# Moving elementwise blocks to GpSimd, all DMA issues to SyncE, and transposing both halves of -u at once, in a chunked linear-attention and MLP kernel

## The chip, the cores and the metric

The kernel runs on one core of one Trainium2 chip. The metric is device time in microseconds (us) of one execution; the median of several runs counts. The engines are called as the profile calls them: PE is TensorE (matmuls; PEld is its weight load), DVE is VectorE, ACT is ScalarE, POOL is GpSimd, SP is SyncE, which here only issues DMAs.

## The reference

There are 4 x 8 heads, a sequence of 768 steps and a head dimension of 40. Each head carries a 40 x 40 state through the sequence, and the heads' outputs, side by side, go through an MLP of 320 -> 2048 -> 320. All data is fp32.

```python
for t in range(S):
    y[:, :, t] = np.einsum('bhd,bhde->bhe', rt, state)
    Sa = np.einsum('bhde,bhe->bhd', state, at)
    state_decay = state * wt[:, :, None, :] - np.einsum('bhd,bhe->bhde', Sa, bt)
    state = state_decay + np.einsum('bhd,bhe->bhde', vt, kt)
...
h = x @ w_in
sp = np.where(h > 20.0, h, np.log1p(np.exp(np.minimum(h, 20.0))))
g = h * np.tanh(sp)
return (g @ w_out).astype(np.float32)
```

## The kernel before

**Chunks.** The sequence is cut into 12 chunks of C = 64 steps (`nch` is 12). Within a chunk the recurrence becomes matrix products and the inverse of a triangular 64 x 64 matrix for each head, so only the state passes from chunk to chunk. The 32 heads are laid out as two halves (`be`), in each of which two groups of 40 dimensions (`al`) stand at partitions 0 and 64, and 8 blocks along the free axis. Steps run over two groups `g` of 4 blocks.

**Preparation, `pre_a(c, be)`**, 24 times. SP loads w and a (`wa`, L322) and b and k (`bk`, L325). DVE forms running products of w forward (`P`, L343) and backward (`E`, L348), scales a (L346), and b and k (L354). ACT copies a into a block form `ad` (L352). PE multiplies `ad` with `bk`, which holds b, k and 40 columns of identity beside them (L386). From PSUM, ACT writes the blocks that couple a with b into `GP` (L389, L391) and the 40 identity columns into `HA` (L393), and DVE writes the 64 columns that couple a with k into `HA` with a triangular mask on the way (L394), then masks `GP` in place (L397). PE transposes b and k (L410) and ACT copies the result to `bkn` (L412). POOL stores `P` to DRAM (L357), since the MLP's input needs it.

**Inverse, `inv(n)`**, once for two chunks. DVE turns the 32 x 32 diagonal blocks (L420), inverts them by 30 pairs of small instructions that depend on each other (L425, L428), and turns the result back (L430, `TT`). PE forms the off-diagonal blocks (L444, L452). ACT copies six blocks for each half into `bdT` (L466, L467 from `TT`, L468 from PSUM), PE multiplies `HA` by `bdT` (L476) and ACT copies the product to `KT` (L479).

**Step, `step(c)`**, in order of the chunks. POOL loads v in two layouts and r (`step_loads`: `VS` L487, `UVT` L491, `bdr` L494). PE forms u from `VS` and `KT` (L514), ACT writes -u into `UVT` beside v (L517). PE multiplies `UVT` by r (L557) and DVE masks that into `UVQ` (L560). PE transposes each half's v and -u (`step_u`, L528, two sets of 4 per group) and ACT copies them into `UVQ` (L530). The state is transposed too (L544) and copied to `smd` (L546). PE then adds up the new state and y (L586, L591), DVE updates the state (L596, L602), ACT copies y (L598) and POOL stores it (L623).

**The MLP** takes pairs of chunks. SP loads y and `P` (L790, L791), and DVE multiplies them. Each operand is split into a high and a low part, and PE does both products (L814, L835 to L837). ACT applies Mish (L817). SP also loads the MLP weights (L728, L731), which DVE and ACT split in spare time.

**Order.** The whole program is a list of operations with an engine, a planned duration, reads and writes. `Plan.order` places them one by one: each engine takes among the operations that could start within a small window (`LOOK`) after the earliest the one with the highest priority. A priority is the length of the work that follows, plus an entry of the table `PRIO` by kind and chunk. Each engine runs its operations strictly in the order found; planned durations affect only this order. Scratch tiles (`HA`, `bkn`, PSUM banks and others) come from pools whose buffers are taken in the same pass. SBUF of the preparation and of the inverse is given to the MLP when they are done, and much of the MLP's storage opens only at the end of the steps.

**Queues.** SP issues the loads of `wa`, `bk`, the constants, the MLP's weights and inputs, and the output. POOL issues all others. Each engine issues in its own order and waits at the head of it.

Of the kernel before, what the change touches and what calls it, by code (L numbers as in the profile page):

```python
# [62 lines left out]
class Plan:
# [183 lines left out]
def attention(actx, tc, I, yD, pD, nch, M, S, newPS):  # L247
    nc = tc.nc
    V, A, PE, SP, G = nc.vector, nc.scalar, nc.tensor, nc.sync, nc.gpsimd
    ictx, pctx = ExitStack(), ExitStack()  # L250
# [65 lines left out]
    def pre_a(c, be):  # L316
        S.at('ld', c)
        wa, bk, ad = wab[be], bkb[be], adb[be]
        xo, og, ok, oa, oh = (0, 0, 64, 0, 40) if be == 0 else (0, 64, 0, 64, 0)
# [30 lines left out]
        for al in range(2):  # L350
            q = slice(al * 64, al * 64 + 64)
            op('A', 0.62, lambda q=q, al=al: A.copy(ad[q, :, :, al], a[q].rearrange("p (s k t) -> p s k t", k=2, t=32)),  # L352
# [528 lines left out]
```

## Time and profile before

| | us |
|---|---|
| median of 3 runs | 747.21 |
| lowest and highest of them | 744.37, 747.24 |
| profiled execution | 745.79 |
| its span | 744.0 |

The profile is one execution. Its page gives the busy time of each engine over the span; the views by line, by window of time, by wait and the chain of work that ended last come from the same trace. A group's row has the line, engine, operation, tiles (out <- in), shapes and count, then busy time, mean ns of one, and the idle time ahead of it with what ended it. Busy bars of PE and DVE overlap their neighbours, so a mean bar is longer than the step from one to the next. The page's slices (40 of 18.6 us, in tenths) show how the load moves:

```profile
PE   2554698999999999999989999999999999999997
DVE  7999999899999999999368853123113113111110
ACT  4554576867887787888858644234334324323332
POOL 9111013142224223212220000000000000000000
PEclk9778589999999999999999999999999999999999
```

### The profile page before, as it was taken

The page shows a single profiled execution, that of the slowest core. Times are in us where ns is not written, and L with a number is a line of the kernel's source. Part 1 is how long each engine was busy: PE and PEld are TensorE (multiplying, and loading weights), DVE is VectorE, ACT ScalarE, POOL GpSimd, SP SyncE. Part 2 cuts the span into 40 slices and gives each one's busy share as a digit, 9 for nine tenths or more (in the row PEclk, how much of TensorE's full clock was granted, in tenths as well). Part 3 has the DMA queues.
Part 4 walks back from the last instruction along what each step waited for, and adds up shares of the span by engine and source line. Part 5 has one row for each costly group of instructions (what it writes and reads, how often), then busy time and mean ns, then how long its engine had stood idle before and what let it go on. Part 6 is the DMA issues. An engine that isn't in the chain of part 4 may idle for free.

```text
span 744.0 us, 17243 instructions
## 1 busy us (share of the span) xinstructions
PE 678.6 (91%) x7048; PEld 626.0 (84%) x7048; DVE 456.0 (61%) x975; ACT 420.8 (57%) x937; POOL 102.2 (14%) x166
## 2 busy tenths in 40 slices
PE   2554698999999999999989999999999999999997
PEld 1544698998999989999978999898998989999897
DVE  7999999899999999999368853123113113111110
ACT  4554576867887787888858644234334324323332
POOL 9111013142224223212220000000000000000000
PEclk9778589999999999999999999999999999999999
DMA  7533214364444445144587713003004001000100
GB/s 191 171 98 89 64 39 104 77 139 116 107 109 111 101 118 150 37 117 128 123 220 185 206 46 100 0 12 97 14 1 103 18 1 40 19 0 1 36 1 35
DMA packets 58206, 61.81 MB, mean 83 GB/s; under 512 B 25536, under 2 KB 48704, under 8 KB 58128
## 3 DMA queue, kind: packets, MB, share of 16 engines
q1 hardware_dynamic: 49296, 40.94, 19.6%
q0 software_dynamic: 8832, 19.79, 10.8%
q8 instruction: 55, 0.90, 0.5%
q14 instruction: 23, 0.19, 0.1%
HBM read 48.79 MB, written 11.86 MB: 82 GB/s over the span
## 4 chain that ended last, share of the span: by engine, by line
PE 64%; DVE 22%; ACT 7%; issue 4%; DMA 1%; POOL 0%; ACTq 0%; DVEq 0%
PE ps L814 24%; PE ps L835 7%; PE ps L837 7%; PE ps L836 7%; PE ps L557 4%; DVE XL L428 3%; DVE tmp L425 3%; PE ps L386 3%; PE ps L586 3%; DVE P L343 2%; DVE bk L354 2%; PE ps L476 2%; PE ps L528 2%; DVE HA L394 2%; PE ps L591 1%
## 5 line engine op out<-in xcount | busy, mean ns | idle before, releaser
L819 DVE TENSOR_TENSOR gl<-g,gh 128x1024 fp32r<-128x1024 f32 x48 | 58.8, 1225 | 194.9 <-ACT gh L818 188.7
L817 ACT ACTIVATE g<-ps 128x512 f32<-128x512 f32 x96 | 57.0, 597 | 173.6 <-PE ps L814 173.3
L837 PE MATMUL ps<-w_oh,gl 128*128 128x320 f32 x384 | 118.6, 309 | 0.0
L835 PE MATMUL ps<-w_oh,gh 128*128 128x320 f32 x384 | 118.5, 309 | 0.0
L836 PE MATMUL ps<-w_ol,gh 128*128 128x320 f32 x384 | 118.5, 309 | 0.0
L814 PE MATMUL ps<-xh,w_ih 128*128 128x512 f32 x288 | 113.2, 393 | 0.0
L814 PE MATMUL ps<-xh,w_il 128*128 128x512 f32 x288 | 97.7, 393 | 0.0
L386 PE MATMUL ps<-bk,ad 128*128 128x168 f32 x384 | 68.7, 340 | 26.9 <-DVE bk L354 18.2
L386 PEld LDWEIGHTS ps<-bk,ad 128*128 128x128 f32 x384 | 63.8, 215 | 28.8 <-issue 26.5
L814 PE MATMUL ps<-xl,w_ih 128*128 128x512 f32 x192 | 75.4, 393 | 0.0
L836 PEld LDWEIGHTS ps<-w_ol,gh 128*128 128x128 f32 x384 | 72.1, 188 | 2.1
L835 PEld LDWEIGHTS ps<-w_oh,gh 128*128 128x128 f32 x384 | 72.1, 188 | 2.0
L837 PEld LDWEIGHTS ps<-w_oh,gl 128*128 128x128 f32 x384 | 72.1, 188 | 0.0
L814 PEld LDWEIGHTS ps<-xh,w_il 128*128 128x128 f32 x288 | 54.1, 188 | 12.3
L814 PEld LDWEIGHTS ps<-xh,w_ih 128*128 128x128 f32 x288 | 54.2, 188 | 10.6 <-issue 0.2
L428 DVE TENSOR_TENSOR XL<-XL,tmp 128x30 f32<-128x30 f32 (+9 forms) x180 | 58.7, 326 | 2.0
L425 DVE TENSOR_TENSOR tmp<-XL 128x30 f32<-128x30 f32 (+9 forms) x180 | 58.5, 325 | 1.7
L557 PE MATMUL ps<-bdr,UVT 128*128 128x128 f32 x384 | 48.8, 283 | 4.9 <-ACT UVT L517 2.7
L818 ACT CAST gh<-g 128x1024 fp32r<-128x1024 f32 x48 | 50.4, 1050 | 1.5
L557 PEld LDWEIGHTS ps<-bdr,UVT 128*128 128x128 f32 x384 | 46.1, 197 | 6.0 <-ACT UVT L517 3.4
L476 PE MATMUL ps<-bdT,HA 128*104 128x128 f32 x384 | 46.9, 280 | 2.4 <-ACT bdT L468 2.4
L476 PEld LDWEIGHTS ps<-bdT,HA 128*104 128x104 f32 x384 | 44.1, 174 | 4.1 <-ACT bdT L468 2.2
(89 smaller groups left out, 1170.9 us busy)
## 6 DMA issues: line engine op xcount, KB each, us to landing
wa<-in_wa SPq DMA_DIRECT2D x48, 162.5 KB
bk<-in_bk SPq DMA_DIRECT2D x48, 160.0 KB
cv<-in_wi SPq DMA_DIRECT2D x12, 512.0 KB
cv<-in_wo SPq DMA_DIRECT2D x8, 640.0 KB
pD<-P POOLq DMA_DIRECT2D x48, 81.2 KB, 2.5
bdr<-in_rD POOLq DMA_DIRECT2D x24, 160.0 KB, 4.5
UVT<-in_vD POOLq DMA_DIRECT2D x24, 160.0 KB, 4.0
VS<-in_vN POOLq DMA_DIRECT2D x24, 160.0 KB, 4.7
```

The source lines that it names most:

```text
L386: PE.matmul(pv()[:, j], ad[:, s0 + j].rearrange("p k a t -> p (k a t)"), bk[:, s0 + j], start=(j == 0), stop=True, skip_group_check=True)
L425: op('V', (0.16 + m * i * 0.00104), lambda tv=tv, i=i, m=m: V.tensor_tensor(out=tv, in0=X[:, i + 1:32, i:i + 1].broadcast_to([128, m, i]), ...
L428: op('V', (0.16 + m * i * 0.00104), lambda tv=tv, i=i: V.tensor_tensor(out=X[:, i + 1:32, 0:i], in0=X[:, i + 1:32, 0:i], in1=tv, op=ALU.ad ...
L476: PE.matmul(kv()[:, j], ha.t[:, s0 + j], bd[:, o + s0 + j].rearrange("p a t -> p (a t)"), start=(j == 0), stop=True, skip_group_check=True)
L557: PE.matmul(qv()[:, s], UVT[:, g * 4 + s, be * 128:be * 128 + 128], bdr[:, be, g * 4 + s].rearrange("p a t -> p (a t)"), start=(s == 0), s ...
L814: PE.matmul(b.t, w, x, start=(n == 0), stop=(n == 7), skip_group_check=True)
L817: op('A', 0.6, lambda b=b, j=j: A.activation(g.t[:, j], b.t, AF.Mish), r=[b], w=[(g, j)])
L818: op('A', 1.05, lambda: A.copy(gh.t, g.t), r=[(g, 0), (g, 1)], w=[gh])
L819: op('V', 1.226, lambda: V.tensor_tensor(out=gl.t, in0=g.t, in1=gh.t.bitcast(F32), op=ALU.subtract), r=[(g, 0), (g, 1), gh], w=[gl])
L835: PE.matmul(o, gh.t[:, j, t], oh, start=(f == 0 and j == 0), stop=False, skip_group_check=True)
L836: PE.matmul(o, gh.t[:, j, t], ol, start=False, stop=False, skip_group_check=True)
L837: PE.matmul(o, gl.t[:, j, t], oh, start=False, stop=(f == 7 and j == 1), skip_group_check=True)
```

## The change

- GpSimd (POOL) makes the copies of a into `ad`, and the four copies from `TT` into `bdT` (per chunk and half). Both were ACT's.
- `HA` is filled from PSUM by one ACT copy of 104 columns per group, unmasked; a POOL instruction then multiplies its 64 columns by the mask, once for 8 blocks. For this, b and k change places in `bk`, so that the identity and k stand side by side. The mask on `GP` moves from DVE to POOL too.
- All DMAs that POOL issued are issued by SP.
- `UVT` gets a new layout in which -u of both halves stands side by side (v0, u0, u1, v1), so that one transpose does both halves; v comes by a further load by time (`vst`, 22 loads) and a POOL copy into `UVQ`. The load of v in the other layout has 9 blocks for 8.
- Transposes take 104 partitions and give 104 columns instead of 128. `smd` gets 344 columns for 4 x 128.
- The planner counts several buffers that an operation needs from one pool. The table of priorities is new, and each kind and chunk gets an addition to the window (`LOOKS`).

```diff
+AD, BD, HM, GM, DM = 'G', 'G', 'G', 'G', 'S'
+LOOKS = {
...
-                        for b in o.bufs:
-                            if b.t is None:
-                                t = max(t, min((f for f in self.free[b.pool[0]] if f is not None), default=1e9))
+                        for name, n in o.wants():
+                            free = sorted(f for f in self.free[name] if f is not None)
+                            t = max(t, free[n - 1] if len(free) >= n else 1e9)
...
+    QD = SP if DM == 'S' else G
+    copy = lambda e: A.copy if e == 'A' else G.tensor_copy
...
+    used = slice(0, 104)
+    rows = cst[used, 0:104]
+    heads = lambda x: bass.AP(x.tensor, x.offset, [x.ap[0], [104, 4], [64, 2], [1, 40]])
...
-            op('A', 0.62, lambda q=q, al=al: A.copy(ad[q, :, :, al], a[q].rearrange("p (s k t) -> p s k t", k=2, t=32)),
+            op(AD, 0.62 if AD == 'A' else 0.86, lambda q=q, al=al: copy(AD)(ad[q, :, :, al], a[q].rearrange("p (s k t) -> p s k t", k=2, t=32)),
...
-            op('G', 0.52, lambda al=al: G.dma_start(out=pD[c, be, :, al], in_=P.t[al * 64:al * 64 + 40]), r=[P], w=[('pD', c, be, al)],
+            op(DM, 0.52, lambda al=al: QD.dma_start(out=pD[c, be, :, al], in_=P.t[al * 64:al * 64 + 40]), r=[P], w=[('pD', c, be, al)],
...
+            if HM == 'G':
+                o = min(oi, ok)
+                op('A', 0.15 + 0.088 * m, lambda s0=s0, m=m, pv=pv, o=o: A.copy(ha.t[:, s0:s0 + m], pv()[:, 0:m, o:o + 104]), r=[b],
+                   w=[(ha, s0), (ha, s0 + 1)])
+                continue
...
+        if HM == 'G':
+            op('G', 1.37, lambda: G.tensor_tensor(out=ha.t[:, :, oh:oh + 64], in0=ha.t[:, :, oh:oh + 64],
+                                                  in1=maskH.unsqueeze(1).broadcast_to([128, 8, 64]), op=ALU.mult), r=['cst'],
+               w=[(ha, s0 + x) for s0 in (0, 3, 6) for x in (0, 1)])
+        op(GM, 0.423 if GM == 'V' else 0.81, lambda: (V if GM == 'V' else G).tensor_tensor(out=gp.t[:, u0:u0 + 8, 1], in0=gp.t[:, u0:u0 + 8, 1],
...
-                    PE.transpose(pv()[:, j].rearrange("p a b -> p (a b)"), bk[:, s0 + j, xo:xo + 128], ident)
+                    PE.transpose(pv()[:, j], bk[used, s0 + j, xo:xo + 128], rows)
...
+                    op(BD, 0.4 if BD == 'A' else 0.56, lambda bd=bd, q0=q0, us=us, al=al: copy(BD)(bd[q0, :, al, 0:32], TT[q0, us]), r=['TT'], w=[bdk[al * 3]])
+                    op(BD, 0.4 if BD == 'A' else 0.56, lambda bd=bd, q1=q1, us=us, al=al: copy(BD)(bd[q1, :, al, 32:64], TT[q1, us]), r=['TT'], w=[bdk[al * 3 + 1]])
...
+            op(DM, 0.75, lambda q=q, al=al: QD.dma_start(out=UVW[q, :, 0:128], in_=I['vD'][c, al].rearrange("p s x t -> p s (x t)")), w=[('UVv', al, 0), ('UVv', al, 1)], lat=2.9, srv=0.85)
...
+            op(DM, 0.85, lambda q=q, al=al: QD.dma_start(out=bdr[q, :, :, al].rearrange("p b s t -> p (b s) t"), in_=I['rD'][c, al]),
...
+    def step_v(c):
+        if c < nch - 1:
+            S.at('sv', c)
+            for be in range(2):
+                q = slice(be * 64, be * 64 + 64)
+                op(DM, 0.65, lambda be=be, q=q: QD.dma_start(out=vst[q], in_=I['vN'][c, be]), w=[('vst', be)], lat=2.3, srv=0.7)
+                op('G', 1.0, lambda be=be, q=q: G.tensor_copy(UVQ[be][q, :, 64:104], vst[q]), r=[('vst', be)], w=[('V', be, 0), ('V', be, 1)])
...
+            def tr():
+                for s in range(4):
+                    PE.transpose(tv()[:, s], UVT[used, g * 4 + s, 64:192], rows)
+            op('P', 0.357, tr, r=[('u', g), 'UVz', 'cst'], w=[b], mode=128, work=0.347)
             for be in range(2):
...
+                src, dst = slice(be * 64, be * 64 + 64), slice(64 - be * 64, 128 - be * 64)
```

More of the change, by code (lines that the diff above doesn't have):

```diff
@@ L20 @@
 LOOK = 0.05
-LOOKS = {}
-PRIO = {
-    'zero': (-99, -65, 338, 745, 81, -91, -72.5, 60, -47.5, -354, -210, 224.5,),
[27 rows of a table removed]
+AD, BD, HM, GM, DM = 'G', 'G', 'G', 'G', 'S'
+LOOKS = {
+    'zero': (1.5,),
[26 rows of a table added]
+}
+PRIO = {
+    'zero': (341.5, 474.5, 514, 250, 460.5, -15, -63.5, -142.5, 9.5, -240.5, -107.5, -174,),
[28 rows of a table added]
 }
@@ L59, with wants @@
 class Op:
-    pass
+    def wants(self):
+        n = {}
+        for b in self.bufs:
+            if b.t is None:
+                n[b.pool[0]] = n.get(b.pool[0], 0) + 1
+        return n.items()
 class Plan:
@@ L283, in attention @@
     VS = tiles(cs, 2, [128, 2, 344], "VS")
-    UVT = cs.tile([128, 8, 256], F32, name="UVT")
+    UVW = cs.tile([128, 9, 256], F32, name="UVT")
+    UVT = UVW.rearrange("p s x -> p (s x)")[:, 64:2112].rearrange("p (s x) -> p s x", x=256)
+    vst = cs.tile([128, 16, 40], F32, name="vst")
     UVQ = tiles(cs, 2, [128, 16, 104], "UVQ")
@@ L304, in attention @@
     UVK = [(k, x, g) for g in range(2) for k, x in (('UVv', 0), ('UVv', 1))] + [('u', g) for g in range(2)]
-    op('G', 2.0, lambda: G.memset(UVT, 0.0), w=UVK)
+    op('G', 2.0, lambda: G.memset(UVW, 0.0), w=UVK + ['UVz'])
     op('G', 2.0, lambda: G.memset(bdr, 0.0), w=[('bdr', al, g) for al in range(2) for g in range(2)])
@@ L310, in attention @@
     op('G', 0.8, lambda: [G.memset(t[:, 640:664], 0.0) for t in S.bkn], w=['bkn0'])
+    op('G', 0.2, lambda: [G.memset(t[:, 320:344], 0.0) for t in S.smd], w=['smd0'])
     view = lambda b, p, n, pat, **k: b.t[p, 0:n].rearrange(pat, **k)
@@ L327, in pre_a @@
             op('S', 0.4, lambda: SP.dma_start(out=cst, in_=I['cst']), w=['cst'], lat=1.8, srv=0.95)
-            for b, t, o in zip(range(2), bkb, (128, 128)):
+            for b, t, o in zip(range(2), bkb, (0, 128)):
                 op('A', 0.42, lambda t=t, o=o: A.copy(t[:, :, o:o + 40], cst[:, 256:296].unsqueeze(1).broadcast_to([128, 8, 40])),
@@ L405, in pre_a @@
             b = newPS()
-            pv = lambda b=b: view(b, full, 512, "p (s a e) -> p s a e", s=4, a=2)
+            pv = lambda b=b: view(b, full, 416, "p (s x) -> p s x", s=4)
             def tr(s0=s0, pv=pv):
                 for j in range(4):
-                    PE.transpose(pv()[:, j].rearrange("p a b -> p (a b)"), bk[:, s0 + j, xo:xo + 128], ident)
-            op('P', 0.44, tr, r=BK + ['cst', 'bkn0'], w=[b], mode=128, work=0.42, claim=[bkn])
-            op('A', 0.43, lambda s0=s0, pv=pv: A.copy(bkn.t[:, s0 * 80:s0 * 80 + 320].rearrange("p (s a e) -> p s a e", a=2, e=40),
-                                                     pv()[:, :, :, 0:40]), r=[b], w=[(bkn, s0)])
+                    PE.transpose(pv()[:, j], bk[used, s0 + j, xo:xo + 128], rows)
+            op('P', 0.357, tr, r=BK + ['cst', 'bkn0'], w=[b], mode=128, work=0.347, claim=[bkn])
+            op('A', 0.43, lambda s0=s0, b=b: A.copy(bkn.t[:, s0 * 80:s0 * 80 + 320].rearrange("p (s a e) -> p s a e", a=2, e=40),
+                                                   heads(b.t)), r=[b], w=[(bkn, s0)])
     def inv(n):
@@ L516, in step_a @@
         op('P', 0.95, mm, r=[(k, g) for k in kts] + [(x, be, g) for x in ('VSv', 'VSs') for be in range(2)], w=[b], lat=0.21, mode=64, work=0.693, cold=0.92)
-        op('A', 0.6, lambda: A.mul(UVT.rearrange("p s (x t) -> p x s t", t=64)[:, 0:4:3, g * 4:g * 4 + 4], uv(), -1.0), r=[b], w=[('u', g)])
+        op('A', 0.6, lambda: A.mul(UVT.rearrange("p s (x t) -> p x s t", t=64)[:, 1:3, g * 4:g * 4 + 4], uv(), -1.0), r=[b], w=[('u', g)])
     def step_u(c, g):
@@ L521, in step_u @@
         if c < nch - 1:
-            for be in range(2):
-                b = newPS()
-                tv = lambda b=b: view(b, full, 512, "p (s a d) -> p s a d", s=4, a=2)
-                def tr(be=be, tv=tv):
-                    for s in range(4):
-                        PE.transpose(tv()[:, s].rearrange("p a d -> p (a d)"), UVT[:, g * 4 + s, be * 128:be * 128 + 128], ident)
-                op('P', 0.44, tr, r=UV(g) + ['cst'], w=[b], mode=128, work=0.42)
-                op('A', 0.43, lambda be=be, tv=tv: A.copy(UVQ[be][:, g * 8:g * 8 + 8, 64:104], tv()[:, :, :, 0:40].rearrange("p s a d -> p (s a) d")),
+            b = newPS()
+            tv = lambda: view(b, full, 416, "p (s x) -> p s x", s=4)
+            def tr():
+                for s in range(4):
+                    PE.transpose(tv()[:, s], UVT[used, g * 4 + s, 64:192], rows)
+            op('P', 0.357, tr, r=[('u', g), 'UVz', 'cst'], w=[b], mode=128, work=0.347)
+            for be in range(2):
+                src, dst = slice(be * 64, be * 64 + 64), slice(64 - be * 64, 128 - be * 64)
+                op('A', 0.43, lambda be=be, src=src, dst=dst: A.copy(UVQ[be][dst, g * 8:g * 8 + 8, 64:104].rearrange("p (s a) d -> p s a d", a=2), heads(b.t)[src]),
                    r=[b], w=[('U', be, g)])
@@ L539, in step_d @@
         smd, b = newSMD(), newPS()
-        dv = lambda: view(b, full, 512, "p (s x) -> p s x", s=4)
+        dv = lambda: view(b, full, 416, "p (s x) -> p s x", s=4)
         def tr():
             for s in range(4):
-                PE.transpose(dv()[:, s], st[:, 2 * s:2 * s + 2].rearrange("p a d -> p (a d)"), ident)
-        op('P', 0.44, tr, r=[('ST', g), 'cst'], w=[b], mode=128, work=0.42)
-        op('A', 0.58, lambda: A.copy(smd.t, dv()), r=[b], w=[smd])
+                PE.transpose(dv()[:, s], st[used, 2 * s:2 * s + 2].rearrange("p a d -> p (a d)"), rows)
+        op('P', 0.357, tr, r=[('ST', g), 'cst'], w=[b], mode=128, work=0.347)
+        op('A', 0.43, lambda: A.copy(smd.t[:, 0:320].rearrange("p (s a d) -> p s a d", a=2, d=40), heads(b.t)), r=[b, 'smd0'], w=[smd])
         return smd
@@ L814, in mm @@
                     PE.matmul(b.t, w, x, start=(n == 0), stop=(n == 7), skip_group_check=True)
-            self.chain(op('P', 1.81, mm, r=[(t, h) for t in (xh, xl) for h in range(2)] + [('wi', q, k) + e for k in range(3) for e in ((), ('l',))],
+            self.chain(op('P', 1.823, mm, r=[(t, h) for t in (xh, xl) for h in range(2)] + [('wi', q, k) + e for k in range(3) for e in ((), ('l',))],
                           w=[b], mode=128, work=1.7, claim=[g, gh, gl]))
```

30 lines of the change are left out of this document (14 added, 16 removed), and 81 rows, old and new, of tables (LOOKS, PRIO).

## The prediction

> **What bounds the kernel now.** I read the page first, then a table of windows cut at the points that the chain of waits shows. The page gives the engines over the whole span:
>
> ```profile
> PE 678.6 (91%) x7048; PEld 626.0 (84%) x7048; DVE 456.0 (61%) x975; ACT 420.8 (57%) x937; POOL 102.2 (14%) x166
> ```
>
> An average over different stages. The chain that ended last, in order of time, says where they are cut (start, length, what; the count is of matmuls):
>
> ```profile
> 85.98 1.92 DVE TT L430
> ...
> 190.91 4.56 PE ps L386 x32
> 195.47 1.78 PE ps L557 x16
> ...
> 208.45 0.87 PE ps L410 x8
> ...
> 211.66 0.87 PE ps L528 x8
> ...
> 380.13 4.46 DMA bdr<-in_rD
> ...
> 393.81 11.10 PE ps L814 x48
> ```
>
> L430 at 86 us is the end of the first triangular inverse: before it no recurrence step can run. From 393.8 to the end the chain is the MLP. The windows between these points (busy time of PE, PEld, DVE, ACT and POOL, then granted clock, DMA share, GB/s):
>
> ```profile
> 0.00:88.00 88.00, 40.45 (x234) 37.77 (x236) 81.06 (x188) 42.66 (x123) 25.38 (x48) 0.78 0.44 121
> 88.00:116.00 28.00, 25.39 (x442) 24.21 (x442) 26.97 (x67) 21.92 (x61) 3.25 (x6) 0.83 0.19 53
> 116.00:345.00 229.00, 221.92 (x3606) 208.86 (x3607) 217.32 (x557) 183.10 (x480) 62.82 (x96) 1.00 0.43 113
> 345.00:394.00 49.00, 44.78 (x851) 42.24 (x851) 29.23 (x56) 36.71 (x81) 9.78 (x14) 0.97 0.58 147
> 394.00:744.00 350.00, 346.09 (x1920) 312.91 (x1919) 101.44 (x111) 136.43 (x196) 1.01 (x2) 1.00 0.17 47
> ```
>
> To 88 us DVE is the bound (81 of 88) and PE idles 48 us. From 116 to 345 both are full: PE idles 7.1 us of 229, DVE 11.7. From 345 to 394 PE is busy 45 of 49. The last 350 us are PE alone, on MLP work that the change leaves as it is. So the total is the first inverse's end, plus the PE work of attention after it, plus the MLP. The change can gain in the first 394 us only. The sum is made against the profiled run's own 745.8 us (span 744.0); the median of the runs is 747.2, 1.4 above.
>
> **The change part by part. DVE.** Both masks leave it: three L394 and one L397 for each prep (chunk and half; 24 preps).
>
> ```profile
> L394 DVE TENSOR_TENSOR HA<-ps,cst 128x192 f32<-128x192 f32 (+1 forms) x72 | 23.1, 327 | 4.9 <-ACT GP L391 3.6 <-ACT GP L389 0.2
> L397 DVE TENSOR_TENSOR GP<-GP,cst 128x256 f32<-128x256 f32 x24 | 9.8, 417 | 1.1 <-ACT GP L389 1.0
> ```
>
> Bars overlap their neighbours, as the timeline of DVE shows, and the windows' counts say how many lie before 88 us:
>
> ```profile
> 77.78 0.35 DVE L394 TENSOR_TENSOR HA<-ps,cst 128x192 f32<-128x192 f32 x1
> 78.05 0.36 DVE L428 TENSOR_TENSOR XL<-XL,tmp 128x210 f32<-128x210 f32 x1
> ...
> L394 DVE TENSOR_TENSOR HA<-ps,cst x24: 280/348/358, 16.7 to 85.1; 128x192 f32<-128x192 f32 x16, 128x128 f32<-128x128 f32 x8
> ...
> L397 DVE TENSOR_TENSOR GP<-GP,cst x7: 396/418/426, 21.7 to 87.9; 128x256 f32<-128x256 f32 x7
> ```
>
> A bar of 0.35 us is followed after 0.27, so each takes its mean less 0.08: 0.247 and 0.337 us. Before 88 us go 24 x 0.247 + 7 x 0.337 = 8.3 us, afterwards 48 x 0.247 + 17 x 0.337 = 17.6 us. In the first stage DVE is the bound, so the first inverse ends **8.3 us** earlier.
>
> **PE.** The transposes run over 104 columns instead of 128, and one per group does both halves of -u, where there were two; v then needs none.
>
> ```profile
> L410 PE MATMUL ps<-cst,bk 128*128 128x128 f32 x192 | 25.4, 282 | 2.4 <-ACT ad L352 2.4
> L528 PE MATMUL ps<-cst,UVT 128*128 128x128 f32 x176 | 22.8, 275 | 1.0 <-ACT UVT L517 1.0
> L544 PE MATMUL ps<-cst,ST 128*128 128x128 f32 x88 | 13.6, 279 | 1.1 <-DVE ST L602 1.1
> ```
>
> Their bars overlap too; the chain gives 0.87 us for 8, so 0.109 each. No transpose of 104 columns is in the trace. Ends: 0.109 (width costs nothing) and 0.109 x 104/128 = 0.0885 (all of it). I take 0.09: in the chain L386 (168 columns) costs 4.56/32 = 0.143 us and L557 (128) 1.78/16 = 0.111, so 0.8 ns a column, 0.019 for 24. L410 saves 192 x 0.019 = 3.6, L544 1.7, L528 176 x 0.109 - 88 x 0.09 = 11.3: 16.6 us, 9.6 at the upper end. About 1.3 of it lies where PE waits for DVE. **15.3** lies after 88 us. There DVE gives up 17.6, more than PE, so PE's relief comes through.
>
> **ACT** loses the copies of a and four of the six block copies of each inverse, and its HA copies grow from 40 to 104 columns.
>
> ```profile
> L352 ACT COPY ad<-wa 64x512 f32<-64x512 f32 x48 | 29.6, 617 | 13.3 <-issue 6.8 <-DVE wa L346 4.6 <-ACT bkn L412 0.9
> L466 ACT COPY bdT<-TT 32x256 f32<-32x256 f32 x48 | 19.4, 403 | 2.0 <-PE ps L476 0.7 <-DVE TT L430 0.5
> L467 ACT COPY bdT<-TT 32x256 f32<-32x256 f32 x48 | 19.2, 401 | 0.9
> L393 ACT COPY HA<-ps 128x120 f32<-128x120 f32 (+1 forms) x72 | 14.7, 240 | 0.4 <-DVE HA L394 0.4
> L479 ACT COPY KT<-ps 104x512 f32<-104x512 f32 x48 | 26.6, 587 | 4.5 <-PE ps L476 3.9
> ```
>
> 68 us go. L393's mean of 107 columns costs 240 ns and L479's 512 cost 587: 0.86 ns a column, times 64 x 8 columns x 24 preps is 10.5 us back. ACT is nowhere the bound, so I count only **1 us**, from PE's waits in the 345-394 stage. If that cover fails, the waits behind ACT return.
>
> **POOL** gets 48 copies of a, 24 + 24 masks, 96 block copies and 22 copies of v, and loses its DMA issues. It has no copy in the trace; the nearest rows are its memsets, and its issues show how good the planner's own entries are:
>
> ```profile
> L309 POOL MEMSET ST<- 128x512 f32 x2 | 1.0, 544 | 0.0
> L494 POOL DMA_DIRECT2D bdr<-in_rD x24 | 20.9, 876 | 38.9 <-PE ps L591 33.7 <-issue 5.2
> L491 POOL DMA_DIRECT2D UVT<-in_vD x24 | 18.1, 754 | 67.1 <-PE ps L557 53.0 <-PE ps L528 14.1
> ```
>
> The entries 0.85 and 0.75 stand beside 0.876 and 0.754, so I take the new ones (0.86, 1.37, 0.81, 0.56, 1.0): 41 + 33 + 19 + 54 + 22 = 169 us over 380. Ends: a memset's rate, under half of that, to three passes at that rate for a mask (1.6 us), some 220 us. POOL has room at either. Longer steps delay the chain to the first inverse: 2 x 0.24 for a, 0.4 for the mask, some waiting; DVE's other preps hide most, I charge **1 us**. Added waits: a mask queues all later POOL work behind it, and L476 waits for HA; that is an inverse later, 20 us or more of DVE work.
>
> **SP** takes 144 issues from POOL and 22 new loads of v.
>
> ```profile
> L322 SPq DMA_DIRECT2D wa<-in_wa x48: 281/287/757, 2.0 to 272.0; - x48
> L325 SPq DMA_DIRECT2D bk<-in_bk x48: 763/764/935, 3.8 to 287.9; - x48
> ```
>
> At 0.3 to 0.8 us each, 166 cost 50 to 130 us of queue, on 59 before (96 such and 20 weight loads): it fits into 390. But POOL's waits (38.9 and 67.1 us in the rows above, for L557 and L591) now stand ahead of the wa and bk loads, whose late arrival stops DVE. One prep takes 229/14 = 16 us of the middle stage, and its load starts as soon as its buffer is free, so some 10 us of delay are covered; charged at nothing. A shorter landing than bdr's 4.46 us could give up to 2 us back.
>
> **Order.** All priorities change and the choice gets a look-ahead. Ends: PE's idle 9.7 us from 88 to 345 recovered, or as much lost; taken at nothing. Also DVE's small copies beside POOL work (below), **1 us**. Sum: 8.3 + 15.3 + 1 - 1 - 1 = 22.6; 745.8 - 22.6 = 723, and with half of the landing and a little of the idle time recovered, **721 us**.
>
> **Rivals. 1, slower: DVE waits for POOL's reads.** DVE and POOL have not computed side by side before. Two rows say that they can hold each other up:
>
> ```profile
> L345 DVE COPY w<-P x24: 159/164/756, 10.5 to 293.9; 128x8 f32<-128x8 f32 x24
> L733 DVE TENSOR_SCALAR cv<-cv x20: 384/486/740, 4.8 to 430.8; 128x512 int32<-128x512 int32 x12, 128x640 int32<-128x640 int32 x8
> ```
>
> The longest L345 (0.756, usually 0.164) stands beside a POOL DMA issue, and ends as the issue ends (timelines of both engines):
>
> ```profile
> 8.98 1.95 POOL L494 DMA_DIRECT2D bdr<-in_rD  x2
> ...
> 10.47 0.76 DVE L345 COPY w<-P 128x8 f32<-128x8 f32 x1
> ```
>
> The instructions that take two inputs from SBUF are the bulk of DVE's work:
>
> ```profile
> L428 DVE TENSOR_TENSOR XL<-XL,tmp 128x30 f32<-128x30 f32 (+9 forms) x180 | 58.7, 326 | 2.0
> L425 DVE TENSOR_TENSOR tmp<-XL 128x30 f32<-128x30 f32 (+9 forms) x180 | 58.5, 325 | 1.7
> L343 DVE TENSOR_TENSOR_SCAN P<-wa,d 128x520 f32<-128x520 f32 x24 | 29.6, 1233 | 0.1
> L354 DVE TENSOR_TENSOR bk<-bk,E 128x1024 f32<-128x1024 f32 x24 | 29.0, 1209 | 0.1
> ```
>
> With L348, a scan like L343, and L346 about 220 us, 0.7 of DVE's 325 us to 345. If a share x of POOL's time is added to DVE, the first stage has 8 preps of 3.9 us on POOL, 31 us, and moves by 31x - 8.3; the middle has 138 and moves by 138x - 17.6 - 11.7 (DVE's idle), never below -15.3. The sum crosses zero at x = 0.22. At x = 0.7 it is +13 + 67: 826 us; at 0.45, 784. Against it: the scans show no long copy (their median is their mean), though next to POOL work that only wrote; and the long L345 shows that a wait, where there is one, can be as long as POOL's instruction. Chance 0.27.
>
> The Trainium skill, page "SBUF — State Buffer", section "Who interferes with whom", speaks against the change: a VectorE instruction with two SBUF inputs contends with a GpSimd instruction that reads SBUF, and the second to start waits for the first to end. By that rule the time is toward this rival's upper end. The trace of before agrees that the two can block each other, with L345's 0.756 us, but has no GpSimd read that could show this case.
>
> **2: the SP queue.** A wait of POOL's kind in front of the loads costs 2 us in each of 12 chunks: 24 us, the whole gain, 745 us. For it: the 38.9 and 67.1 us above; against it: the cover of 10 us. Chance 0.08.
>
> **3: only PE's part arrives, and at its upper end**: POOL's longer steps or the new order hold the first inverse where it is, and narrower transposes cost no less each. 9.6 - 1.3 = 8.3 us remain: 737 us. For it: the 0.4 us longer mask right ahead of the inverse; against it: DVE is full to 88 us, and what it gives up there is its own work. Chance 0.10.
>
> **How the numbers follow.** The forecast has 0.55, with its own range 706 to 736 (the order's 10 us, and the transposes' 7 above and the landing and POOL's end at a memset's rate, some 5, below). Faster: 0.55 + 0.10 = 0.65, same 0.08, slower 0.27. "Same" is within 0.5%, about what a measurement of this kernel can tell from no change. The range reaches from 704 into rival 1, to x near 0.4, 775 us; beyond lie some 0.15, below some 0.03.
>
> **What would show it.** Right: L430's first end near 80 us, first MLP matmul near 370, 88 transposes for -u of 0.09 us in the chain, PE idle in the middle stage still under 10. Rival 1: L425 and L428 longer than their 325 ns while POOL computes. Rival 2: DVE idle before L341 or L354, ended by a DMA. Wrong altogether would be an MLP stage other than 350 us.

## The result and the profile after

| | before | after |
|---|---|---|
| median, us | 746.74 (4 runs) | 777.99 (4 runs) |
| lowest and highest, us | 744.37, 747.24 | 772.56, 780.65 |
| profiled execution, us (span) | 745.79 (744.0) | 780.65 (778.8) |

The changed kernel is slower by 4.2%: the ratio is 1.0416, with an interval of 1.0355 to 1.0476. The time lies just above the predicted range (704 to 775), and a gain had been forecast (721). The profiled run of the changed kernel is the slowest of its four, 2.7 us above their median.

Line numbers move with the change: L425 and L428 (the inverse's pairs) are now L480 and L483, L430 is L485, L343 and L348 (the scans) are L389 and L394, L345 is L391, L346 is L392, L354 is L400, L557 is L621, L560 is L624, L528 is L590, L410 is L465 and L814 is L879. On POOL, L398 copies a, L449 masks `HA`, L452 masks `GP`, L521 and L522 copy into `bdT`, and L558 copies v.

The page of the changed kernel first, busy time of each engine:

```profile
PE 673.4 (86%) x6960; PEld 622.8 (80%) x6960; DVE 486.5 (62%) x879; ACT 358.9 (46%) x793; POOL 184.8 (24%) x238
```

DVE executes 96 instructions fewer (879 for 975) and is busy 30.5 us longer (486.5 for 456.0). The 96 masks that left are worth 33 us of bars. So the bars of what stayed must have grown by more than 60 us over the whole span. The chain of the changed kernel shows where the stages are cut (start, length, what):

```profile
67.38 1.92 DVE TT L485
...
428.62 11.11 PE ps L879 x48
```

The first inverse ends at 69.3 us, 18.6 us earlier than before (87.9). Yet the first MLP matmul starts at 428.6, 34.8 us later than before. The windows between these points (busy time of PE, PEld, DVE, ACT and POOL, clock, DMA share, GB/s) say that the middle lost it:

```profile
0.00:69.00 69.00, 18.54 (x112) 17.73 (x112) 57.29 (x112) 19.36 (x56) 31.24 (x44) 0.74 0.42 112
69.00:116.00 47.00, 38.85 (x554) 37.28 (x555) 45.67 (x74) 25.91 (x76) 33.52 (x34) 0.87 0.42 116
116.00:380.00 264.00, 227.12 (x3545) 214.62 (x3544) 247.56 (x525) 145.53 (x398) 110.95 (x142) 0.92 0.38 105
380.00:428.60 48.60, 42.54 (x834) 40.04 (x832) 30.30 (x54) 30.71 (x65) 9.07 (x18) 0.96 0.60 158
428.60:778.80 350.20, 346.31 (x1922) 313.12 (x1920) 105.68 (x118) 137.38 (x201) 0.00 (x0) 1.00 0.18 49
```

To the first inverse's end DVE is now busy 57 us, where it was 81 up to the same point; and the last two stages are as before (48.6 for 49, and 350.2 for 350). The middle takes 264 us instead of 229. That is not all of it, since its start at 116 us lies 47 us behind the first inverse now and 28 before: from the first inverse's end to the MLP it is 359.3 us for 305.9, 53 more. In the middle DVE is busy 247.6 of 264 us and idle 16; PE is idle 37, where it was idle 7, and its granted clock is 0.92 instead of 1.00. So DVE sets the pace there, and PE waits. DVE's costliest groups up to there, with mean ns of one behind the comma:

```profile
L483 DVE TENSOR_TENSOR XL<-XL,tmp 128x30 f32<-128x30 f32 (+9 forms) x180 | 76.1, 423 | 2.8
L480 DVE TENSOR_TENSOR tmp<-XL 128x30 f32<-128x30 f32 (+9 forms) x180 | 71.4, 397 | 2.9
...
L394 DVE TENSOR_TENSOR_SCAN E<-wa,d 128x519 f32<-128x519 f32 x24 | 32.4, 1349 | 0.2
L389 DVE TENSOR_TENSOR_SCAN P<-wa,d 128x520 f32<-128x520 f32 x24 | 31.9, 1329 | 0.9 <-DMA pD<-P 0.7
```

The same instructions on the same shapes took 326, 325, 1230 and 1233 ns before. The timelines of DVE and POOL show what a lengthened one looks like:

```profile
163.23 1.21 DVE L400 TENSOR_TENSOR bk<-bk,E 128x1024 f32<-128x1024 f32 x1
...
163.32 2.25 POOL L449 TENSOR_TENSOR HA<-HA,cst 128x512 f32<-128x512 f32 x1
164.36 1.28 DVE L483 TENSOR_TENSOR XL<-XL,tmp 128x58 f32<-128x58 f32 x1
```

POOL's mask is issued while DVE's L400 runs; its bar is 2.25 us, about 1 us over its usual length, and that is the rest of L400. Then L483 on 58 columns stands at 1.28 us and ends at 165.64, where the mask ends (165.57). Here each waits for the rest of the other's instruction, in the order in which they started. By tile, minimum, median and maximum in ns:

```profile
L480 DVE TENSOR_TENSOR tmp<-XL x180: 158/370/1341, 44.4 to 377.4; 128x30 f32<-128x30 f32 x12, 128x58 f32<-128x58 f32 x12, 128x84 f32<-128x84 f32 x12, 128x108 f32<-128x108 f32 x12
...
L398 POOL COPY ad<-wa x48: 600/666/1689, 9.6 to 317.6; 64x512 f32<-64x512 f32 x48
L449 POOL TENSOR_TENSOR HA<-HA,cst x24: 1257/1394/2250, 20.8 to 346.3; 128x512 f32<-128x512 f32 x24
L452 POOL TENSOR_TENSOR GP<-GP,cst x24: 719/732/1652, 20.0 to 340.7; 128x256 f32<-128x256 f32 x24
L521 POOL COPY bdT<-TT x48: 386/392/1478, 69.4 to 395.9; 32x256 f32<-32x256 f32 x48
L522 POOL COPY bdT<-TT x48: 393/399/1444, 69.8 to 396.4; 32x256 f32<-32x256 f32 x48
L558 POOL COPY UVQ<-vst x22: 709/785/1597, 17.9 to 387.9; 64x640 f32<-64x640 f32 x22
```

The minima say what POOL's work costs undisturbed: 48 x 0.600 + 24 x 1.257 + 24 x 0.719 + 48 x 0.386 + 48 x 0.393 + 22 x 0.709 = 129 us. The maxima of both engines lie about one instruction of the other engine above them.

This is what rival 1 described, and the page of the Trainium skill named there, "SBUF — State Buffer", section "Who interferes with whom", describes it too. But that is not yet a price: the SP queue, the new order and the longer steps changed in the same edit. The experiments take them apart.

### The profile page after: what moved, and what is told of

Same layout as the page of the kernel before. It is cut to its first block, busy times and chain, and to the rows that moved or that the text cites. A ratio compares the mean times of both kernels' runs of the same rounds, so it can differ in the third digit from the quotient of the medians.

```text
span 778.8 us, 17122 instructions
## 1 busy us (share of the span) xinstructions
PE 673.4 (86%) x6960; PEld 622.8 (80%) x6960; DVE 486.5 (62%) x879; ACT 358.9 (46%) x793; POOL 184.8 (24%) x238
## 4 chain that ended last, share of the span: by engine, by line
PE 61%; DVE 25%; issue 5%; DMA 4%; ACT 1%; POOL 1%; SPq 1%; DVEq 0%; ACTq 0%; POOLq 0%
PE ps L879 23%; PE ps L902 7%; PE ps L900 7%; PE ps L901 7%; DVE XL L483 6%; DVE tmp L480 6%; PE ps L621 5%; PE ps L531 2%; PE ps L432 2%; PE ps L577 2%; DVE bk L400 2%; DMA wa<-in_wa 1%; DVE wa L392 1%; PE ps L465 1%; DVE UVQ L624 1%
## 5 line engine op out<-in xcount | busy, mean ns | idle before, releaser
L879 PE MATMUL ps<-xh,w_ih 128*128 128x512 f32 x288 | 113.2, 393 | 0.0
L879 PE MATMUL ps<-xh,w_il 128*128 128x512 f32 x288 | 97.7, 393 | 0.0
L483 DVE TENSOR_TENSOR XL<-XL,tmp 128x30 f32<-128x30 f32 (+9 forms) x180 | 76.1, 423 | 2.8
L879 PE MATMUL ps<-xl,w_ih 128*128 128x512 f32 x192 | 75.4, 393 | 0.0
L480 DVE TENSOR_TENSOR tmp<-XL 128x30 f32<-128x30 f32 (+9 forms) x180 | 71.4, 397 | 2.9
L879 PEld LDWEIGHTS ps<-xh,w_il 128*128 128x128 f32 x288 | 54.1, 188 | 12.3
L879 PEld LDWEIGHTS ps<-xh,w_ih 128*128 128x128 f32 x288 | 54.2, 188 | 10.6 <-ACT yev L662 0.2
L621 PE MATMUL ps<-bdr,UVT 128*128 128x128 f32 x384 | 52.5, 300 | 3.6 <-DMA bdr<-in_rD 3.0
L621 PEld LDWEIGHTS ps<-bdr,UVT 128*128 128x128 f32 x384 | 50.1, 214 | 4.7 <-issue 3.4
L398 POOL COPY ad<-wa 64x512 f32<-64x512 f32 x48 | 42.9, 894 | 28.4 <-PE ps L414 8.0
```

Source lines behind the costliest of these rows:

```text
L480: op('V', (0.16 + m * i * 0.00104), lambda tv=tv, i=i, m=m: V.tensor_tensor(out=tv, in0=X[:, i + 1:32, i:i + 1].broadcast_to([128, m, i]), ...
L483: op('V', (0.16 + m * i * 0.00104), lambda tv=tv, i=i: V.tensor_tensor(out=X[:, i + 1:32, 0:i], in0=X[:, i + 1:32, 0:i], in1=tv, op=ALU.ad ...
L621: PE.matmul(qv()[:, s], UVT[:, g * 4 + s, be * 128:be * 128 + 128], bdr[:, be, g * 4 + s].rearrange("p a t -> p (a t)"), start=(s == 0), s ...
L879: PE.matmul(b.t, w, x, start=(n == 0), stop=(n == 7), skip_group_check=True)
```

## The experiments

The theory, A: POOL's reads of SBUF and DVE's instructions with two SBUF inputs exclude each other, and this costs all of what was lost. The rival, B: transfers behind SP's queue, or the new order, cost it. Medians are in us; each ratio is against runs of the kernel before on the same chip (medians 747.02 to 747.19; the changed kernel's own comparison had 746.74).

| run | what it is | median | ratio (interval) |
|---|---|---|---|
| e1 | after, POOL writes and doesn't read | 725.74 | 0.971 (0.968 to 0.975) |
| e2 | before, with 144 POOL copies | 821.48 | 1.100 (1.098 to 1.103) |
| e3 | before, with 144 POOL memsets | 752.12 | 1.007 (1.005 to 1.009) |
| e4 | after, POOL's work back, order planned anew | 807.95 | 1.081 (1.074 to 1.087) |
| e5 | after, DMA issues back on POOL | 788.42 | 1.056 (1.053 to 1.060) |
| e6 | after, copies on ACT, order held | 777.33 | 1.041 (1.038 to 1.045) |
| e7 | after, masks on DVE, order held | 768.45 | 1.031 (1.027 to 1.034) |
| e8 | after, both, order held | 773.92 | 1.037 (1.034 to 1.040) |
| e9 | before, with narrow transposes | 745.08 | 0.998 (0.996 to 1.000) |
| e10 | before's order, PE's part alone | 752.76 | 1.006 (1.004 to 1.009) |
| e11 | after, masks read, copies only write | 750.97 | 1.003 (1.000 to 1.006) |

**e1: POOL's reads taken away, its place and time kept.** Every POOL copy and mask becomes memsets of the same tile, so values are lost, and waits and order stay. A mask becomes two memsets, to come near its length.

```diff
-            op(AD, 0.62 if AD == 'A' else 0.86, lambda q=q, al=al: copy(AD)(ad[q, :, :, al], a[q].rearrange("p (s k t) -> p s k t", k=2, t=32)),
+            op(AD, 0.62 if AD == 'A' else 0.86, lambda q=q, al=al: G.memset(ad[q, :, :, al], 0.01),
...
-            op('G', 1.37, lambda: G.tensor_tensor(out=ha.t[:, :, oh:oh + 64], in0=ha.t[:, :, oh:oh + 64],
-                                                  in1=maskH.unsqueeze(1).broadcast_to([128, 8, 64]), op=ALU.mult), r=['cst'],
+            op('G', 1.37, lambda: [G.memset(ha.t[:, :, oh:oh + 64], 0.01)
+                          for _ in range(2)], r=['cst'],
```

> The changed kernel with every GpSimd copy and mask replaced by memsets of the same blocks (masks twice), so that GpSimd only writes; the copies of a, of the inverse's blocks and of v and both masks are left out. Every engine's order is that of the changed kernel. Theory A (DVE's instructions with two SBUF inputs wait for GpSimd instructions that read SBUF): the means of the inverse's two groups fall from 397 and 423 ns to 325 and 326, DVE's busy time falls by some 45 us, the last inverse ends near 340 instead of 380 us, and the time is 725 to 745 us. Theory B (the single SP queue and the new order hold the work up): DVE's bars may shorten, but the time stays above 765 us.

Measured: 725.74 us, 52 us below the changed kernel. The page of e1, and the two groups of its lines:

```profile
PE 655.1 (90%) x6960; PEld 607.8 (84%) x6960; DVE 436.7 (60%) x879; ACT 359.4 (50%) x793; POOL 117.0 (16%) x286
...
L483 DVE TENSOR_TENSOR XL<-XL,tmp 128x30 f32<-128x30 f32 (+9 forms) x180 | 59.0, 328 | 2.8
L480 DVE TENSOR_TENSOR tmp<-XL 128x30 f32<-128x30 f32 (+9 forms) x180 | 59.0, 328 | 2.9
```

POOL is still busy 117 us, at the same places; only the reads are gone. DVE's pairs are back at 328 ns and DVE's busy time falls by 486.5 - 436.7 = 49.8 us, nearly all of the 52. SP's queue, the transposes and the new order are unchanged, and with them the kernel is 21 us faster than before: B has nothing left to explain. A stands, and the reads cost 52 us for 129 us of undisturbed POOL time: 0.40. Two things differ besides: the memsets are somewhat shorter than what they replace (108 of the 117 us, for 129), and the values are not the kernel's. The MLP stage took 350.6 us with these values and 350.2 without.

**e2 and e3: the same in the kernel before.** A POOL instruction on spare tiles is put behind each of POOL's 144 DMA issues: in e2 a copy, in e3 a memset of as many columns. Order and everything else stay as before. One of the five places, first e2, then e3:

```diff
-            op('G', 0.52, lambda al=al: G.dma_start(out=pD[c, be, :, al], in_=P.t[al * 64:al * 64 + 40]), r=[P], w=[('pD', c, be, al)],
+            op('G', 0.52, lambda al=al: [G.dma_start(out=pD[c, be, :, al], in_=P.t[al * 64:al * 64 + 40]), G.tensor_copy(dmy[0], dmy[1])], r=[P], w=[('pD', c, be, al)],
```

```diff
+            op('G', 0.52, lambda al=al: [G.dma_start(out=pD[c, be, :, al], in_=P.t[al * 64:al * 64 + 40]), G.memset(dmy[0], 0.0)], r=[P], w=[('pD', c, be, al)],
```

> The kernel before, with one GpSimd copy of 128 x 512 from one idle tile to another behind each of GpSimd's 144 DMA issues; no other engine's order is changed. Some 0.6 us each, 86 us of reads. Theory A: each copy stops DVE for a good part of its length: inverse groups 380 ns instead of 325, time 765 to 785 us. Theory B: nothing but slightly later DMA issues, the same as the twin with memsets, 745 to 753 us.

> The twin of the run with copies: one GpSimd memset of 128 x 512 (0.54 us) behind each of the 144 DMA issues of the kernel before, no reads. Both theories: 745 to 753 us, the inverse groups at 325 to 335 ns. If it is as slow as the copies, then GpSimd's time itself or the later DMA issues cost, and not its reads.

Measured: 821.48 with copies, 752.12 with memsets. By line, in e2:

```profile
L425 DVE TENSOR_TENSOR tmp<-XL 128x30 f32<-128x30 f32 (+9 forms) x180 | 78.5, 436 | 1.8
L428 DVE TENSOR_TENSOR XL<-XL,tmp 128x30 f32<-128x30 f32 (+9 forms) x180 | 77.6, 431 | 2.0
```

and in e3:

```profile
L428 DVE TENSOR_TENSOR XL<-XL,tmp 128x30 f32<-128x30 f32 (+9 forms) x180 | 59.2, 329 | 2.0
L425 DVE TENSOR_TENSOR tmp<-XL 128x30 f32<-128x30 f32 (+9 forms) x180 | 58.7, 326 | 1.8
```

The memsets cost 5 us and leave DVE's pairs alone; the copies cost 74 and make them a third longer, which is more than A had expected (765 to 785 us, 380 ns). This is the Trainium skill's distinction in the section named above: a VectorE instruction with two SBUF inputs contends with GpSimd's reads, and not with its writes. Both runs agree. An undisturbed copy took 0.623 us here, so 144 of them are 90 us of reads, and the twin's difference of 69 us is 0.77 of it: more than the 0.40 of e1. DVE is fuller with the masks on it, and the copies come wherever a DMA is issued; that this is the reason is not shown.

**e4: POOL's arithmetic back on DVE and ACT, order planned anew.** The kernel's own switches do it; PE's part, SP's queue and the tables stay.

```diff
-AD, BD, HM, GM, DM = 'G', 'G', 'G', 'G', 'S'
+AD, BD, HM, GM, DM = 'A', 'A', 'V', 'V', 'S'
```

> The changed kernel with the copies back on ScalarE and the masks back on VectorE (the order is planned anew with the same priorities); SP still issues all DMAs, one transpose still does both halves of -u, and only the 22 copies of v stay on GpSimd. Theory A: DVE's two-input groups return to 325 ns within 10 ns, and PE's 15 us saving shows: 725 to 740 us. Theory B (SP's queue): 750 to 775 us, with DVE or PE idle ended by DMAs.

Measured: 807.95. Neither theory gave that. In its lines the pairs are near their old length, and new waits stand behind the bar (L445 is L394 before, the mask on `HA`):

```profile
L483 DVE TENSOR_TENSOR XL<-XL,tmp 128x30 f32<-128x30 f32 (+9 forms) x180 | 61.0, 339 | 2.5
L480 DVE TENSOR_TENSOR tmp<-XL 128x30 f32<-128x30 f32 (+9 forms) x180 | 61.0, 339 | 2.5
...
L624 DVE TENSOR_TENSOR UVQ<-ps,cst 128x512 f32<-128x512 f32 x48 | 32.5, 686 | 28.6 <-PE ps L621 28.4
...
L445 DVE TENSOR_TENSOR HA<-ps,cst 128x192 f32<-128x192 f32 (+1 forms) x72 | 23.3, 329 | 22.6 <-PE ps L432 13.4 <-ACT GP L437 8.2 <-ACT HA L444 0.2
```

The lock is nearly gone, and DVE waits 51 us at these two lines instead, where the kernel before waited some 10. The priorities of the changed kernel were made for its own durations and engines; with others the same table seems to give a poor order, which no run tests by itself. A switch in this kernel doesn't change one thing. The next four runs (e5 to e8) therefore keep the planned durations and engines, so the order is the changed kernel's, and only the engine that executes is exchanged.

**e5: the DMA issues that moved to SP go back to POOL's queue**, order of the other engines held.

```diff
-QD = SP if DM == 'S' else G
+QD = G
```

> The changed kernel with the 166 moved DMA issues back on GpSimd's queue, every other instruction in the changed kernel's order. Theory A (reads of GpSimd stop DVE; 52 us of the changed kernel's time by the run with memsets): the queue is not the cause, 770 to 795 us, since the reads stay and GpSimd gets longer work in front of them. Theory B (a part of the loss is the single SP queue): below 768 us.

Measured: 788.42, ten us slower than the changed kernel. The pairs take 419 and 411 ns, as in the changed kernel. So SP's queue isn't what cost the time; in this order, taking the issues off POOL was worth 10 us.

**e6, e7 and e8: the copies, the masks, and both, taken off POOL, order held.** The first edit, with the same for the copies into `bdT` and `UVQ`, makes e6; the second, with the same for `GP`, makes e7; both make e8.

```diff
-            op(AD, 0.62 if AD == 'A' else 0.86, lambda q=q, al=al: copy(AD)(ad[q, :, :, al], a[q].rearrange("p (s k t) -> p s k t", k=2, t=32)),
+            op(AD, 0.62 if AD == 'A' else 0.86, lambda q=q, al=al: A.copy(ad[q, :, :, al], a[q].rearrange("p (s k t) -> p s k t", k=2, t=32)),
...
-            op('G', 1.37, lambda: G.tensor_tensor(out=ha.t[:, :, oh:oh + 64], in0=ha.t[:, :, oh:oh + 64],
+            op('G', 1.37, lambda: V.tensor_tensor(out=ha.t[:, :, oh:oh + 64], in0=ha.t[:, :, oh:oh + 64],
```

> The changed kernel with the copies of a, of the inverse's blocks and of v on ScalarE instead of GpSimd, each at its place in the changed kernel's order; the masks stay on GpSimd. About 48 us of GpSimd reads are left of 129. Theory A, 0.4 us of time lost for each us of reads: 726 + 19 = 745 us, 738 to 755. Were the copies harmless and the two-input masks the cause: 770 us or more.

> The changed kernel with both masks on VectorE instead of GpSimd (two SBUF inputs, at their place in the changed kernel's order); the copies stay on GpSimd, about 82 us of reads. Theory A: DVE gets 22 us of masks back and loses 33 us to the copies instead of 52: 726 + 33 + 15 to 22, 770 to 785 us. Were the masks the cause and the copies harmless: 740 to 750 us.

> The changed kernel with the copies on ScalarE and the masks on VectorE, all at their places in the changed kernel's order: no computing on GpSimd, SP issues all DMAs, one transpose for both halves of -u. Theory A: no lengthened DVE group (inverse 325 to 330 ns); DVE gets 22 us of masks back: 726 + 12 to 22, 738 to 750 us. Theory B (the SP queue and the order are the loss): 765 us or more.

Measured: 777.33, 768.45 and 773.92. The expectations of A for e6 (738 to 755) and e8 (738 to 750) failed, and e7 lies between its two (740 to 750, 770 to 785). For e8 the time is even the one that B gave (765 or more). Against SP's queue as the reason stand e1 and e5; the order is left. With e8 nothing of POOL's reads is left, and its DVE groups show that:

```profile
L480 DVE TENSOR_TENSOR tmp<-XL 128x30 f32<-128x30 f32 (+9 forms) x180 | 58.7, 326 | 2.7
L483 DVE TENSOR_TENSOR XL<-XL,tmp 128x30 f32<-128x30 f32 (+9 forms) x180 | 58.7, 326 | 2.7
L624 DVE TENSOR_TENSOR UVQ<-ps,cst 128x512 f32<-128x512 f32 x48 | 32.3, 686 | 31.1 <-PE ps L621 16.0 <-ACT bdT L523 6.0 <-ACT UVT L580 4.7
```

The pairs are at their old 326 ns, and waits took the lock's place: 31.1 us at L624 alone, 15.2 in the changed kernel. In e6 it is the same (29.4 us there, 21.4 of it for PE's L621): DVE is busy 30 us less than in the changed kernel (456.3 for 486.5), and the time is no shorter. In e7 the masks lock no more and their work is DVE's again; the copies still lengthen the pairs, to 370 and 365 ns. In e6 and e8 ACT is busy 83 us longer than in the changed kernel (442 for 359), in an order that was found without them, so what it delivers to PE and DVE comes late. That ACT's order is the cause is argued from the releasers; no run had an order made for this split of the work, so it isn't shown. What these three do show is that the work can't simply be given back in this order.

**e9 and e10: what PE's part is worth by itself.** e9 narrows 368 transposes in the kernel before and touches nothing else.

```diff
-PE.transpose(pv()[:, j].rearrange("p a b -> p (a b)"), bk[:, s0 + j, xo:xo + 128], ident)
+PE.transpose(pv()[:, j].rearrange("p a b -> p (a b)")[:, 0:104], bk[0:104, s0 + j, xo:xo + 128], ident[0:104, 0:104])
...
-PE.transpose(tv()[:, s].rearrange("p a d -> p (a d)"), UVT[:, g * 4 + s, be * 128:be * 128 + 128], ident)
+PE.transpose(tv()[:, s].rearrange("p a d -> p (a d)")[:, 0:104], UVT[0:104, g * 4 + s, be * 128:be * 128 + 128], ident[0:104, 0:104])
```

> The kernel before with one edit: the 192 transposes of L410 and the 176 of L528 run over 104 columns; order and all else as before. If width is paid for (0.8 ns a column) and TensorE alone limits the middle stage, 368 x 0.0185 = 6.8 us come off: 740 us, and the bars' spacing falls from 0.109 to 0.09. If VectorE, busy 217 of 229 us there, limits it as much, under 2 us come off: 745 to 747 us, with the spacing at 0.09 and TensorE's idle time grown by what it saves. If width costs nothing: 747 us with the spacing at 0.109.

Measured: 745.08, 2.1 us below before (ratio 0.9979, 0.996 to 0.9997). The chain before at two places, the chain of e9 at the same two, and e9's window of the middle stage:

```profile
189.89 1.02 PE ps L528 x8
197.26 0.87 PE ps L528 x8
```

```profile
189.72 0.86 PE ps L528 x8
196.95 0.72 PE ps L528 x8
```

```profile
116.00:342.00 226.00, 216.30 (x3597) 203.27 (x3598) 215.90 (x556) 179.96 (x478) 62.99 (x96) 1.00 0.43 113
```

Eight transposes take 0.15 or 0.16 us less at each place, 0.019 for one, and 0.09 each where they took 0.109. PE's work in the middle falls by 221.9 - 216.3 = 5.6 us, the stage by 3, in the one execution that is profiled, which is e9's fastest (742.21); PE's idle time grows from 7.1 to 9.7. DVE is busy 215.9 of 226 us there, so it can hardly let more through.

e10 takes the merged and narrow transposes and the load of v by time into the order of the kernel before, with all else where it was; only the 22 copies of v are POOL's. Each engine's order is read from a list, that of the kernel before with the operations of `step_v` put in.

```diff
-AD, BD, HM, GM, DM = 'G', 'G', 'G', 'G', 'S'
+AD, BD, HM, GM, DM = 'A', 'A', 'V', 'V', 'G'
...
-                    if o.eng == e:
+                    if held[e] and o.i == held[e][-1]:
...
-                op(DM, 0.65, lambda be=be, q=q: QD.dma_start(out=vst[q], in_=I['vN'][c, be]), w=[('vst', be)], lat=2.3, srv=0.7)
+                op('S', 0.65, lambda be=be, q=q: SP.dma_start(out=vst[q], in_=I['vN'][c, be]), w=[('vst', be)], lat=2.3, srv=0.7)
```

> TensorE's part of the change alone, in the order of the kernel before: one narrow transpose for both -u, v loaded by time on SP's queue and copied by POOL (22 copies); masks back on VectorE, copies of a and of the inverses back on ScalarE, the other transfers back on POOL's queue. TensorE loses 16.6 us of work, POOL gains 22 x 0.71 = 15.6 us of reads, worth 6 us at the 0.4 that the reads cost in the changed kernel (52 of 129 us). If TensorE's relief comes through by itself: 747 - 15 + 6 = 738 us. If it needs VectorE's relief, which is not there: 745 to 753 us, TensorE's idle time in the middle grown from 7 to some 20 us.

Measured: 752.76, slower than before by 0.6% (0.4 to 0.9%). The windows of e10, the middle stage being its first and the end of the steps its second line; the profiled execution is the slowest of the ten (756.43):

```profile
116.00:355.00 239.00, 217.92 (x3588) 202.44 (x3590) 225.16 (x560) 182.36 (x484) 80.30 (x116) 0.99 0.46 121
355.00:404.00 49.00, 43.37 (x792) 40.85 (x787) 28.01 (x54) 34.78 (x77) 10.96 (x16) 0.90 0.65 158
```

DVE's busy time in the middle grows from 217.3 to 225.2 us, though it got no work: its pairs went from 325 to 344 and 346 ns, 7 us in all, beside 22 x 0.709 = 15.6 us of undisturbed copies (0.45 of it). PE is idle 21 us instead of 7. So PE's relief didn't come through where DVE was not relieved. That DVE alone is the reason isn't shown: the waits that are named for PE there end with ACT's -u (L561) for 6.6 us and with DVE for 5.9, and the loads of v and their copies are new in this run.

**e11: masks read, copies only write.** It divides the 52 us. The copies of a, of the inverses and of v become memsets as in e1, and the masks stay.

> The changed kernel with the copies of a, of the inverses and of v replaced by memsets of the same tiles (they no longer move data), the two masks still read; order as in the changed kernel. The masks are 47 of POOL's 129 us of reads. If blocked time goes with the time read: 726 + 52 x 47/129 = 745 us. If it goes with length squared (a longer instruction is met more often and its rest is longer: masks 51, copies 43 in us squared): 726 + 28 = 754 us.

Measured: 750.97, between the two figures (745 and 754), nearer to the one by length squared; the run doesn't decide it. Its two groups:

```profile
L480 DVE TENSOR_TENSOR tmp<-XL 128x30 f32<-128x30 f32 (+9 forms) x180 | 66.9, 372 | 2.9
L483 DVE TENSOR_TENSOR XL<-XL,tmp 128x30 f32<-128x30 f32 (+9 forms) x180 | 65.5, 364 | 2.8
```

Against e1 the masks' reads cost 25 us (for 47 us of undisturbed time), and the copies' reads the other 27 (for 82 us). Leaving DVE, the masks had freed 8.3 + 17.6 = 26 us. By this sum moving the masks gave back what it took, and the copies, which freed only ACT, were a loss. The runs in the held order bear out the first half (e7 is even 9.5 us faster than the changed kernel) and not the second (e6 is as slow as it).

No version that was run beats the kernel before by more than e9's 0.2%, which is within what a measurement of this kernel can tell. e1 is faster, but leaves POOL's part of the computation out.

## Why the prediction was wrong, by its steps

- **What failed is the term "DVE's small copies beside POOL work", at 1 us.** The forecast charged DVE's whole life beside POOL at 1 us; it cost 52 (after against e1). Those 52 us make the difference between 726 and 778. Rival 1 had the mechanism, and the sign given for it came (the pairs took 397 and 423 ns for 325 and 326). The range, cut at x near 0.4, fell 3 us short.
- **Rival 1's price was near by luck.** Its formula reaches the profiled run's +34.8 us at 169x = 72.4, x = 0.43, and it gave 784 us at 0.45. But POOL's 169 us were 129, and the share that e1 measures is 0.40 of those; with both, 129 x 0.40 - 37.6 is +14, or 760 us. It took off 37.6 us for what DVE gives up and for its idle time, where e1 shows a gain of 21 without the reads. It also had the first inverse later (31 x 0.43 - 8.3 = 5 us), and it came 18.6 us earlier.
- **Why it was held too unlikely.** Against the rival stood "the scans show no long copy (their median is their mean), though next to POOL work that only wrote". Writes were taken as half a piece of evidence, and e3 beside e2 shows that they are none. The clause after "though" should have voided the argument. What was left spoke for the rival: the rule of the Trainium skill that the prediction names has exactly the pair that the change makes. The rule holds here, as the twin e2 and e3 shows.
- **L345's 0.756 us was read wrongly,** and was weaker evidence than it looked. It ends at 11.23 us, in the middle of a later issue (L491), and the issue named beside it had ended at 10.93. DVE lost nothing by it: the next instruction starts 0.08 us after it, as usual, and has its usual length (0.684). So this row didn't show the block that the prediction took from it.

```profile
10.55 0.69 DVE L346 TENSOR_TENSOR wa<-wa,P 128x512 f32<-128x512 f32 x1
...
10.92 1.42 POOL L491 DMA_DIRECT2D UVT<-in_vD  x2
```

- **POOL's time** was estimated at 169 us and is 129 undisturbed, below each planner's entry (0.60 for 0.86, 1.26 for 1.37, 0.72 for 0.81, 0.39 for 0.56, 0.71 for 1.0). With the lock it is 175. Two ends were summed a little wrong, and nothing rests on them: at a memset's rate (0.544 us for 512 columns) the same work is 87 us, just over half of 169, and the forecast's own upper end is 721 + 10 + 7 = 738, and not 736.
- **The rest of the sum held as a sum, and partly by luck.** e1 has everything but the reads and takes 725.7, 4.7 above 721. Its parts are not the forecast's: its first inverse ends at 66.2 us, 21.7 earlier (8.3 forecast), and from there to the MLP it takes 309 us, 3 longer than before (15.3 shorter forecast). It also has what SP's issues gain, which the forecast put at nothing. PE's relief alone gave 2 of 6.8 us in e9, and nothing in e10. This fits the prediction's "There DVE gives up 17.6, more than PE, so PE's relief comes through", but no run frees DVE by itself.
- **The first inverse** was expected 8.3 us earlier and came 18.6 earlier. DVE was busy 24 us less up to it (57.3 for 81.1). Masks are 8.3 of them. The rest is work that the new order puts after it (four L400 lie ahead of the first inverse's end, where eight L354 lay), and postponing gains nothing by itself.
- **Transposes:** 88 for -u instead of 176, as said, and 0.09 us each in the chain of e9. In the changed kernel the chain has 12 of b and k (L465) in 1.07 us at 100 us, 0.089 each, where the granted clock is 1.00, and 12 in 2.08 us at 256 us, 0.17 each, where it is 0.50.
- **SP's queue at nothing:** right that it costs nothing, wrong that it gains nothing. The longest waits of DVE for `wa` are 6.1 us in two, but e5 shows the issues better on SP by 10 us, a gain that the forecast didn't have. Rival 2 falls with e5.
- **Order at nothing:** can't be separated. In e4, e6 and e8, where the lock is smaller or gone and the work is on other engines than those the order was made for, the time is about as long as with the lock or longer; that the order is what costs it there is argued.
- **MLP stage:** 350.2, as said.

## What to carry to other kernels

Before elementwise work goes to GpSimd, list VectorE's instructions with two SBUF inputs beside it. VectorE was near its limit here, each microsecond of GpSimd's reads cost 0.4 to 0.8, and what moving the masks freed on VectorE (26 us) was given back by their own reads (25 us). GpSimd was nearly free for what only writes (5 us for 144 memsets). When two engines are both full, don't add their reliefs: in e9 and e10 that of TensorE alone hardly came through. And when a planner's order is tuned to durations, test a part by exchanging the engine with the order held, knowing that the held order then has a price of its own.
